# A new written order, new engine choices and new buffer places for the same 24-group attention and expert kernel

## The chip, the cores and the metric

The kernel runs on one core of one Trainium2 chip. The metric is device microseconds of one execution on that core; the times before are given as the median of three runs. Names of engines: PE multiplies matrices, DVE (VectorE), ACT (ScalarE) and POOL (GpSimd) work elementwise, SP only issues transfers here. A matmul's result lies in PSUM (8 banks); PE writes PSUM, DVE and ACT read it, POOL works on SBUF alone.

## The reference, cut to what matters

```python
def _attn_ref(x, inducing):              # x: 4 x 11456 x 128, inducing: 32 x 128
    def mab(q, kv):
        s = scale * (q @ kv.transpose(0, 2, 1))
        s = s - s.max(-1, keepdims=True)
        a = np.exp(s)
        a /= a.sum(-1, keepdims=True) + 1e-09
        return a @ kv
    h = mab(I, x)                         # 32 rows per batch
    return mab(x, h).astype(np.float32)

def _moe_ref(x, expert_emb, tau, w1, w2):  # x: the 45824 x 128 result above
    logits = xn @ en.T / tau              # xn, en: rows of norm 1
    expert_idx = np.argmax(logits, axis=1)
    probs = softmax(logits); gate_w = probs[arange, expert_idx]
    for e in range(8):
        mask = expert_idx == e
        h = np.maximum(x[mask] @ w1[e], 0.0)
        out[mask] = gate_w[mask, None] * (h @ w2[e])
```

## The kernel before, in words

Each of the 4 batches is cut into 6 groups of 1,920 tokens, so there are 24 groups, 0 to 23; groups 0 to 5 are batch 0, and so on. All of a batch's tokens turn out to take one expert, which the kernel finds from a vote and reads as a whole; a verdict at the end looks at whether that held, and a slow loop behind it (not run here) does the work otherwise.

Stage 1 of a group g: `load g` brings the tokens with channels on partitions. A second form of the same tokens, tokens on partitions, comes either by a second transfer (`loadx g`, 12 of the groups) or by transposes on PE (`xt g.0`, `xt g.1`) and their copies out of PSUM (`xe g.0`, `xe g.1`). `s1` are the scores on PE, `e1` their exp on ACT, `e1t` a transpose on DVE, `h` the accumulation of the batch's 32 rows on PE.

After a batch's sixth `h` come the small steps of `finish`: `zc, zr, rz, hsb, hd, hdc, tab, tabc, vote, pick`, then `loadw` (1 MB of the chosen expert's weights by two transfers, whose address `pick` gives), and with the weights `G, GT, gs, gk, K, Kc, K4, K4c`. `tabs`, `ad`, `md`, `mdc`, `marg`, `mq`, `mx`, `h2`, `zk` and `ck1` to `ck5` serve the gate and the verdict.

Stage 2 goes over pairs of groups (named by the first, 0, 2, ... 22). For each group: `s2` (scores, PE), `am` (maximum, DVE), `e2` (exp, ACT), `ud` (PE), `w` (product, DVE or POOL, with `uc` as a copy for POOL). Then one chain for the pair: `n2` and `dt` (DVE), `ln, ex` (ACT), `z, fac` (POOL), `den` (DVE), `lg` (POOL), `el` (ACT), `S` (DVE), `v` (POOL), `gf` (the gate's reciprocal, on DVE as two instructions or on ACT as three). With the gate each group's output follows: `F` (DVE spreads the gate), `eg` (product, POOL or DVE), `out` (four matmuls in two PSUM pairs), `oe .0` and `oe .1` (copies of 960 columns each out of PSUM, ACT or DVE) and `store` (SP, 960 KB). Groups 18, 22 and 23 do this in two parts (`F 22.0`, `eg 22.0`, `out 22.0`, `oe 22.0.0`, `oe 22.0.1`, `store 22.0`, and `.1`), whose copies have 512 and 448 columns.

No scheduler moves anything. `ORDER` (lines 58 to 113) is the list of all steps; each engine executes its own steps in that order, and a quote mark behind a name takes the second of the step's possible engines. `SEATS` gives each tile its place among 18 large, 5 middle and 10 small buffers and 8 PSUM banks. A step waits for its inputs and for the former users of its place. `FILL` puts matmuls on zeros ahead of some PE steps, so many to a PSUM bank (line 709). A `load` or `loadx` also waits for the fifth one before it:

```python
DEPTH = 5
            if op.paced:
                if len(paced) >= DEPTH:
                    tc.add_manual_dep(op.insts[0].ins, paced[-DEPTH].insts[-1].ins.name,
```

Of the kernel before, what the change touches and what calls it, by code (L numbers as in the profile page):

```python
# [63 lines left out]
hdc 0', shd 1, s1 9, s2 0, xe 9.0, tab 0, tabc 0, s2 5, vote 0, am 0, pick 0, sta 0, stb 0, load 11, tabs 0.0,
tabs 0.1, tabs 0.2, s2 4, e1 6, e1 9, stc 0, std 0, e2 0, load 10, s2 1, tabs 0.3, am 5, tabs 0, e1t 9, e2 1, am 1,
s2 2, e2 2, ud 0, ud 2, e2 4, uc 0, ud 1, am 2, s1 10, e1 10, w 0, ad 0, s2 3, load 7, pad 23, am 4, e1t 6, e2 5,
w 1, h2 0, s1 7, n2 0, md 0, pad 11, dt 0, e2 3, ln 0, ex 0, mdc 0, z 0, e1t 10, load 8, pad 17, am 3, loadx 6,
e1 7, load 12, loadw 0, ud 4, w 4, fac 0, uc 2, den 0, ud 3, dt 2, ud 5, w 5, dt 4, lg 0, z 2, loadx 7, el 0, S 0,
xt 11.0, xe 11.0, w 3, e1t 7, n2 4, xt 10.0, xe 10.0, v 0, gf 0, F 0, w 2, n2 2, eg 0, xt 12.1, xe 12.1, xt 11.1,
xt 9.1, xe 9.1, zk 0, F 1, z 4, xt 10.1, xe 10.1, loadx 8, ln 2, ex 2, s1 8, e1 8, G 0, h 6, GT 0, ln 4, gs 0,  # L70
s1 11, fac 2, den 2, h 7, lg 2, e1t 8, s1 12, load 16, load 20, h 8, gk 0, marg 0.0, el 2, S 2, K 0, ex 4, fac 4,
den 4, lg 4, e1 11, load 14, marg 0.1, el 4, m1 12, ck1 0, marg 0, xe 11.1', eg 1, mq 0, h 9, Kc 0, sha 2, shb 2,
e1t 11, K4 0, h 10, K4c 0, mx 0, shc 2, ck2 0, shd 2, load 13, v 2, h 11, gf 2, S 4, v 4, ck3 0, hsb 1, zc 1, zr 1,
rz 1.0, rz 1, F 2, e1 12, load 15, out 0, oe 0.1, F 3, hd 1, s1 14, load 17, hdc 1', tab 1, gf 4', e1t 12, out 1,
e1 14, tabc 1', vote 1, oe 0.0, loadx 16, F 4, s2 6, store 0, s2 9, pick 1, F 5, tabs 1.0, tabs 1.1, am 6, s2 10,
oe 1.0, oe 1.1, eg 2', eg 5, eg 4, sta 1, stb 1, am 9, s1 13, loadw 1, stc 1, std 1, s2 8, h2 1, e1t 14, e2 9, e2 6,
s2 11, am 11, e2 10, e2 8, s2 7, e2 7, e2 11, tabs 1.2, am 8, tabs 1.3, tabs 1, s1 15, eg 3, am 7, am 10, xt 17.0,
xe 17.0, ud 8, w 8, e1 13, ad 1, e1t 13, ud 6, loadx 14, w 6, ud 9, dt 8, ud 7, e1 15, uc 7, out 2, s1 16, md 1,
oe 2.1, w 9, oe 2.0, n2 8, G 1, ln 8, ex 8, w 7, z 8, e1 16, n2 6, loadx 13, dt 6, mdc 1, ud 10, w 10, z 6, fac 8,
den 8, load 18, e1t 15, GT 1, gs 1, xt 12.0, marg 1.0, gk 1, xe 12.0, lg 8, xt 17.1, xe 17.1, ln 6, ud 11, w 11,  # L80
loadx 15, marg 1.1, el 8, zk 1, out 3, oe 3.1, marg 1, e1t 16, S 8, h 12, mq 1, store 1, v 8, ex 6, s1 17, dt 10,
fac 6, h 13, oe 3.0, den 6, n2 10, K 1, gf 8, F 8, lg 6, mx 1, F 9, ck1 1, out 4, oe 4.1, Kc 1', oe 4.0', h 14,
s1 18, load 23, el 6, h 15, e1 17, K4 1, store 2, out 5, eg 9, S 6, zc 2, eg 8, h 16, ln 10, K4c 1, ex 10, oe 5.0,
ck2 1, e1t 17, m1 18, v 6, z 10, fac 10, den 10, lg 10, gf 6, sha 3, shb 3, zr 2, rz 2.0, ck3 1, rz 2, oe 5.1, h 17,
hsb 2, F 6, eg 6, load 22, loadx 22, shc 3, shd 3, el 10, S 10, loadx 19, e1 18, store 5, xt 18.0, xe 18.0, v 10,
hd 2, hdc 2', s1 23, tab 2, tabc 2', s2 12, F 7, vote 2, out 6, am 12, pick 2, gf 10, e1 23, s2 17, sta 2, load 19,
tabs 2.0, tabs 2.1, tabs 2.2, e1t 23, tabs 2.3, oe 6.0, stb 2, tabs 2, e1t 18, s2 14, hde 3, loadw 2, load 21, eg 7,
stc 2, oe 6.1, std 2, e2 12, am 17, am 14, s2 15, e2 15, F 10, eg 10, e2 14, F 11, eg 11, s2 16, e2 17, ad 2, am 15,
s2 13, am 13, s1 20, e2 16, am 16, out 7, e1 20, ud 12, e1t 20, e2 13, oe 7.0, oe 7.1, store 7, ud 14, uc 14, ud 13,
w 12, ud 15, w 13, w 15, dt 14, out 8, oe 8.1, w 14, oe 8.0, z 14, s1 19, s1 22, n2 14, ln 14, ex 14, n2 12, ln 12,  # L90
ex 12, dt 12, G 2, GT 2, h2 2, z 12, fac 12, zk 2, fac 14, md 2, mdc 2, gs 2, ud 16, xt 18.1, den 12, e1 22,
marg 2.0, lg 12, den 14, e1 19, w 16, xe 18.1, e1t 19, marg 2.1, el 12, S 12, marg 2, mq 2, xt 23.1, xe 23.1,
xt 23.0, xe 23.0, ud 17, v 12, lg 14, gf 12', out 9, gk 2, F 13, e1t 22, F 12, mx 2, dt 16, loadx 21, loadx 20,
store 3, h 18, oe 9.0, store 6, eg 13', store 8, oe 9.1, s1 21, e1 21, el 14, h 19, out 10, w 17, oe 10.0, e1t 21,
S 14, h 20, v 14, gf 14, n2 16, eg 12', K 2, Kc 2, h 21, oe 10.1, ln 16, out 11, oe 11.0, F 15, eg 15, h 22,
oe 11.1', K4 2, K4c 2', zc 3, ex 16, z 16, fac 16, h 23, hsb 3, zr 3, rz 3.0, den 16, rz 3, store 9, lg 16, el 16,
out 13, oe 13.1, F 14, store 10, oe 13.0, hd 3, hdc 3', tab 3, S 16, store 11, v 16, gf 16, s2 18, tabc 3', vote 3,
out 12, oe 12.1, oe 12.0, eg 14', am 18, sta 3, store 4, pick 3, stb 3, tabs 3.0, F 16, tabs 3.1, s2 21, stc 3,
std 3, tabs 3.2, am 21, tabs 3.3, tabs 3, s2 19, am 19, eg 16', e2 18, e2 21, s2 20, F 17, am 20, e2 19, ud 18,
uc 18, w 18, e2 20, loadw 3, store 12, ud 19, w 19, store 13, dt 18, n2 18, eg 17, out 14, oe 14.0, ln 18, ud 20,  # L100
w 20, z 18, zk 3, ud 21, w 21, oe 14.1, store 14, dt 20, z 20, n2 20, out 15, ex 18, G 3, s2 22, GT 3, fac 18,
den 18, lg 18, oe 15.0, oe 15.1, s2 23, store 15, ad 3, gs 3, ln 20, out 16, am 23, e2 22, ex 20, fac 20, am 22,
el 18, e2 23, S 18, gk 3, v 18, oe 16.1, oe 16.0, den 20, lg 20, ud 22, w 22, gf 18', F 19, F 18.1, F 18.0, ud 23,
# [776 lines left out]
```

## Time and profile before

| | |
|---|---|
| median of three runs | 166.08 us (165.87 to 166.93) |
| the profiled execution's own time | 166.93 us |
| its span, first to last instruction | 165.2 us |
| busy PE, DVE, ACT, POOL | 154.0, 125.3, 114.9, 53.0 us |
| moved on SP's queue | 62.92 MB, 95.4% of 16 DMA engines' span |

The profiled execution is the slowest of the three, 0.85 us over the median; 1.73 us of its own time lie outside the span. Busy times are of each engine alone and overlap; a matmul's end is modelled, so a busy PE says that matmuls stood ready and not that PE was at its peak.

### The profile page before, as it was taken

Reading aid. Unit: us, or ns where it says so; the run is one execution under the profiler, and the core shown is the slowest. Engines: PE = TensorE matmul, PEld = TensorE weight load, DVE = VectorE, ACT = ScalarE, POOL = GpSimd, SP = SyncE. Lnnn points to the kernel's source line nnn. Section 1 sums busy time; section 2 is a strip of 40 time slices with the busy share of each in tenths; the row PEclk is TensorE's granted clock in tenths of the full one; section 3 lists DMA queues with packets and bytes.
Section 4 is the critical chain, followed back from the end, with each engine's and each line's share of the span. In section 5 each row is a group of like instructions: output and inputs, shape, how many; then the busy total and the mean of one; then the engine's idle time right before and its main releaser. Section 6 shows DMA issues by size and latency. Waiting matters only on the chain.

```text
span 165.2 us, 5835 instructions
## 1 busy us (share of the span) xinstructions
PE 154.0 (93%) x2351; PEld 82.6 (50%) x2351; DVE 125.3 (76%) x323; ACT 114.9 (70%) x238; POOL 53.0 (32%) x148
## 2 busy tenths in 40 slices
...
GB/s 159 421 424 427 411 415 411 415 426 406 413 398 337 348 415 420 420 415 415 426 397 417 411 390 293 314 354 413 417 418 419 281 429 413 372 397 392 413 405 72
DMA packets 10574, 63.34 MB, mean 384 GB/s; under 512 B 1320, under 2 KB 1328, under 8 KB 10544
## 3 DMA queue, kind: packets, MB, share of 16 engines
q1 hardware_dynamic: 10368, 62.92, 95.4%
...
## 4 chain that ended last, share of the span: by engine, by line
PE 77%; DVE 12%; ACT 3%; POOL 2%; issue 1%; POOLq 0%; ACTq 0%
PE psum L304 62%; PE psum L406 12%; DVE big L301 2%; DVE sml L629 2%; ACT big L301 2%; PE psum L709 2%; POOL sel L276 2%; DVE gf L616 1%; PE psum L374 1%; ACT E L425 1%; DVE n L590 1%; DVE sum L612 1%; DVE sml L631 1%; DVE sml L429 0%; ACT mid L554 0%
## 5 line engine op out<-in xcount | busy, mean ns | idle before, releaser
L301 ACT COPY big<-psum 128x960 f32<-128x960 f32 (+4 forms) x67 | 58.7, 913 | 13.6 <-PE psum L304 9.2
L304 PE MATMUL psum<-sml,K 32*128 32x480 f32 (+2 forms) x216 | 26.7, 566 | 1.0 <-POOL z L603 0.7
L304 PE MATMUL psum<-big,sml 128*32 128x128 f32 x720 | 27.0, 274 | 0.0
L304 PEld LDWEIGHTS psum<-big,sml 128*32 128x32 f32 x720 | 22.6, 110 | 8.7 <-issue 4.2
L631 POOL TENSOR_TENSOR sml<-mid,sml 128x480 f32<-128x480 f32 (+2 forms) x18 | 20.4, 1147 | 19.5 <-DVE sml L629 9.9
L304 PE MATMUL psum<-big,ind 128*32 128x480 f32 x192 | 25.4, 571 | 0.0
L406 PE MATMUL psum<-ident,big 128*128 128x128 f32 x180 | 23.0, 282 | 0.2
L425 ACT ACTIVATE E<-psum,nb 128x480 f32<-128x480 f32 (+2 forms) x28 | 18.2, 652 | 6.6 <-PE psum L304 6.1
L406 PEld LDWEIGHTS psum<-ident,big 128*128 128x128 f32 x180 | 20.1, 144 | 4.9 <-issue 1.6
L304 PE MATMUL psum<-mid,tD 32*32 32x480 f32 x192 | 22.5, 569 | 0.0
L304 PE MATMUL psum<-mid,tab 32*32 32x480 f32 x192 | 22.5, 569 | 0.0
L304 PE MATMUL psum<-big,hd 128*32 128x480 f32 x192 | 22.3, 568 | 0.0
L429 DVE STREAM_TRANSPOSE sml<-E 128x480 f32<-128x480 f32 x24 | 15.9, 664 | 7.1 <-ACT E L425 7.1
L568 POOL TENSOR_TENSOR mid<-sml,mid 128x480 f32<-128x480 f32 x6 | 7.3, 1210 | 42.0 <-ACT sml L301 42.0
L554 ACT ACTIVATE mid<-psum,nb 128x480 f32<-128x480 f32 x24 | 14.5, 660 | 4.3 <-DVE nb L377 3.8
L550 DVE TENSOR_REDUCE am<-psum 128x1 f32<-128x480 f32 x24 | 15.2, 647 | 2.6 <-PE psum L304 2.0
L629 DVE STREAM_TRANSPOSE sml<-gf 128x480 f32<-128x480 f32 (+2 forms) x27 | 15.7, 600 | 0.0
L568 DVE TENSOR_TENSOR mid<-psum,mid 128x480 f32<-128x480 f32 x18 | 11.5, 638 | 3.3 <-PE psum L304 3.1
L304 PEld LDWEIGHTS psum<-sml,K 32*128 32x128 f32 x216 | 8.6, 183 | 10.7 <-ACT big L301 2.6
L590 DVE TRANSPOSE_TENSOR_REDUCE n<-mid 128x30 f32<-128x960 f32 x12 | 13.7, 1148 | 0.1
L709 PE MATMUL psum<-zero 128*128 128x256 bf16 x66 | 11.4, 312 | 1.7 <-DVE zero L260 1.0
L301 DVE COPY big<-psum 128x960 f32<-128x960 f32 (+4 forms) x11 | 10.4, 954 | 1.1 <-PE psum L304 0.8
...
## 6 DMA issues: line engine op xcount, KB each, us to landing
...
```

The source lines that it names most:

```text
L301: return nc.scalar.copy(out, in_) if e == "ACT" else ENG[e].tensor_copy(out, in_)
L304: return nc.tensor.matmul(out, lhsT=lhsT, rhs=rhs, start=start, stop=stop)
L406: return [nc.tensor.transpose(ap(tp)[:, (q - q0) // 4, 128 * ((q - q0) % 4):128 * ((q - q0) % 4) + 128], v(q), ident) for q in range(q0, q1)]
L425: return [nc.scalar.activation(ap(e1)[r0:r1, :n], ap(ps)[r0:r1, :n], AF.Exp, bias=bt.t("nb")[r0:r1, 0:1], scale=SCALE, accum_out=bt.t("zk" ...
L429: add(f"e1t {g}", ("DVE",), lambda e: [nc.vector.transpose(ap(e1t), ap(e1))], [e1], [e1t])
L550: add(f"am {g}", ("DVE",), lambda e, ps=ps, k=k: [v.tensor_reduce(t("am")[:, k:k + 1], ap(ps)[:, :W], AX.X, ALU.max, apply_absolute_value= ...
L554: add(f"e2 {g}", ("ACT",), lambda e, ps=ps, a=a: [nc.scalar.activation(ap(e2)[:, a], ap(ps)[:, :W], AF.Exp, bias=t("nb")[:, 1:2], scale=SC ...
L568: return [ENG[e].tensor_tensor(ap(wp)[:, a], src(), ap(e2)[:, a], ALU.mult)]
L590: add("n2 " + nm, ("DVE",), lambda e: [v.tensor_reduce(fl2(u("n2")), ap(wp).rearrange("p a (q i) -> p (a q) i", i=32), AX.X, ALU.add, appl ...
L629: add(f"F {nm}", ("DVE",), lambda e, a=a, f=f, q0=q0, q1=q1: [v.transpose(ap(f).rearrange("p (q i) -> p q i", i=32)[:, q0:q1], u("gf")[:, ...
L631: add(f"eg {nm}", ("POOL", "DVE"), lambda e, a=a, f=f, e2g=e2g, c0=c0, c1=c1: [ENG[e].tensor_tensor(ap(e2g)[:, c0:c1], ap(e2)[:, a, c0:c1] ...
L709: fill = [nc.tensor.matmul(psum[:, s, 0:256], lhsT=zero[:, 0:P], rhs=zero, start=True, stop=True) for _ in range(n)]
```

## The change

`ORDER`, `SEATS` and `FILL` are replaced; the set of steps, `LOADED`, `W_POOL`, `SPLIT`, `DEPTH` and all functions stay. SP issues the same 72 transfers in another order. 41 steps change engine: `eg 2, 12, 13, 14, 16, 22.0, 23.0, 23.1` go from DVE to POOL and `eg 4` from POOL to DVE; `gf 0, 8, 16, 20`, `K4c 0, 1, 3`, `hsb 3`, `oe 0.1, 22.0.0, 22.1.1` and seven `xe` from ACT to DVE; `en7`, `gf 12`, `hdc 1`, `tabc 1, 2`, `oe 4.0, 18.0.0, 21.1, 23.0.0, 23.1.0, 23.1.1` and three `xe` from DVE to ACT. The fill matmuls are 72 instead of 66.

The last lines of the new list and the new fills, as they stand in the diff (two lines of the list, then the table of fills):

```diff
+oe 22.0.0', marg 3, oe 21.0, store 21, eg 23.1, mq 3, out 22.1, oe 22.0.1, oe 22.1.0, out 23.1, oe 23.1.1,
+store 22.0, oe 22.1.1', eg 23.0, out 23.0, ck4 1, ck5 1, mx 3, oe 23.1.0, store 23.1, ck2 3, store 22.1, ck3 3,
...
 FILL = {
-    "xt 0.1": (0, 16), "xt 0.0": (2, 3), "tab 3": (2, 4), "ud 19": (2, 2), "ud 21": (0, 2), "ud 23": (3, 2),
-    "K4 3": (0, 5), "out 18.0": (0, 6), "out 20": (4, 3), "out 21": (2, 5), "out 22.0": (4, 8), "out 22.1": (6, 4),
-    "out 23.0": (4, 5), "ck4 3": (2, 1),
+    "xt 0.1": (0, 16), "s1 0": (2, 3), "ud 17": (2, 2), "tab 3": (4, 4), "out 15": (4, 2), "ud 23": (2, 2),
+    "K4 3": (0, 5), "out 18.0": (0, 3), "out 19": (0, 3), "out 21": (2, 9), "out 22.0": (6, 14), "out 23.0": (2, 3),
+    "ck2 3": (4, 3), "ck4 3": (0, 3),
 }
```

What the instructions of three engines are, in a row, at the places that the prediction comes to. In these rows `sml<-gf` is `F`, `sml<-mid,sml` is `eg`, `n<-mid` is `n2`, `gf<-v` is `gf`, `big<-psum` is `oe`, `den<-s` is `den`, `K<-psum` is `K4c`; the numbers behind names are places.

DVE, from the copy of `K` or the last pair's `n2` on, before:

```order
L590 TENSOR_REDUCE n_125<-mid_85 128x30
L629 STREAM_TRANSPOSE sml_96<-gf_113 128x480
L301 COPY big_78<-psum 128x2x8x32
L486 TENSOR_REDUCE chk_123<-tab_117 128x1
L629 STREAM_TRANSPOSE sml_90<-gf_113 128x480
L655 TENSOR_REDUCE chk_123<-am_119 128x1
L656 TENSOR_REDUCE chk_123<-n_125 128x1
L606 RECIPROCAL den_102<-s_100 128x30
```

and after the change:

```order
L301 COPY K_122<-psum 128x128
L629 STREAM_TRANSPOSE sml_91<-gf_113 128x480
L616 RECIPROCAL gf_105<-v_104 64x30 x2
L629 STREAM_TRANSPOSE sml_95<-gf_105 128x480
L590 TENSOR_REDUCE n_125<-mid_85 128x30
L655 TENSOR_REDUCE chk_123<-am_119 128x1
L656 TENSOR_REDUCE chk_123<-n_125 128x1
L301 COPY big_82<-psum 128x2x15x32
L606 RECIPROCAL den_110<-s_108 128x30
```

The copy of `K`, the gate `gf 20` and `F 20` now stand ahead of the last pair's `n2 22`; before, they stood behind it or on ACT.

POOL, the last steps, before:

```order
L631 TENSOR_TENSOR sml_92<-mid_83,sml_96 128x480
L608 TENSOR_TENSOR lg_106<-sml_93,den_102 128x240
L613 TENSOR_TENSOR v_104<-sum_103,z_101 128x30
L631 TENSOR_TENSOR sml_89<-mid_84,sml_88 128x224
L531 TENSOR_TENSOR q_163<-q_163 128x16
```

and after:

```order
L613 TENSOR_TENSOR v_112<-sum_111,z_109 128x30
L631 TENSOR_TENSOR sml_88<-mid_84,sml_96 128x256
L631 TENSOR_TENSOR sml_88<-mid_84,sml_96 128x224
L454 COPY chk_123<-zc_151 128x1
L454 TENSOR_SCALAR chk_123<-zc_151 128x1
L631 TENSOR_TENSOR sml_91<-mid_84,sml_93 128x224
L531 TENSOR_TENSOR q_163<-q_163 128x16
L631 TENSOR_TENSOR sml_91<-mid_84,sml_93 128x256
```

Behind `v 22` POOL had one half product (`eg 22.1`); now it has all four halves of groups 22 and 23, and the two instructions of `zk 3`.

SP, the last five stores, before (`store 21` has 1920 columns; then `22.1, 23.0, 22.0, 23.1`):

```order
L644 DMA out_0<-big15_80 128x1920
L644 DMA out_0<-big7_72 128x896
L644 DMA out_0<-big5_70 128x1024
L644 DMA out_0<-big7_72 128x1024
L644 DMA out_0<-big5_70 128x832
```

and after (`22.0, 23.1, 22.1, 23.0`):

```order
L644 DMA out_0<-big12_77 128x1920
L644 DMA out_0<-big1_66 128x1024
L644 DMA out_0<-big10_75 128x832
L644 DMA out_0<-big1_66 128x896
L644 DMA out_0<-big10_75 128x1024
```

`store 22.1` stood ahead of both stores of group 23; now it stands between them.

## Rows read from the trace of the kernel before

**Rows 1.** The page: busy times, GB/s in 40 slices, SP's queue.
```profile
PE 154.0 (93%) x2351; PEld 82.6 (50%) x2351; DVE 125.3 (76%) x323; ACT 114.9 (70%) x238; POOL 53.0 (32%) x148
...
GB/s 159 421 424 427 411 415 411 415 426 406 413 398 337 348 415 420 420 415 415 426 397 417 411 390 293 314 354 413 417 418 419 281 429 413 372 397 392 413 405 72
...
q1 hardware_dynamic: 10368, 62.92, 95.4%
```
**Rows 2.** Windows: stretch, length, busy us of each engine, PEclk, DMA share, GB/s.
```profile
4.75:135.40 130.65, 130.26 (x2110) 71.53 (x2114) 102.79 (x255) 95.82 (x203) 39.42 (x91) 1.00 1.00 397
...
38.50:49.20 10.70, 10.70 (x166) 7.47 (x162) 10.19 (x21) 9.33 (x21) 5.00 (x12) 1.00 1.02 412
49.20:53.00 3.80, 3.80 (x107) 3.30 (x102) 3.68 (x13) 3.01 (x12) 2.23 (x4) 1.00 0.90 340
...
125.50:159.40 33.90, 30.05 (x354) 11.26 (x346) 30.79 (x87) 25.59 (x49) 12.69 (x23) 1.00 0.99 389
150.40:159.40 9.00, 5.99 (x63) 3.03 (x55) 7.82 (x30) 3.73 (x7) 0.90 (x2) 1.00 1.00 410
...
133.60:163.40 29.80, 21.95 (x253) 9.16 (x237) 23.55 (x67) 19.28 (x38) 9.80 (x19) 0.94 0.94 380
```
**Rows 3.** Timeline of SP's issues: start and us of the last store's issue.
```profile
158.52 0.33 SPq L644 DMA_DIRECT2D out<-big  x1
```
**Rows 4.** Line 644 at 158.52: the last store, from issue to landing.
```profile
DMA to landing us min/median/max: 4.9/4.9/4.9
```
**Rows 5.** Timeline of PE: start, us, and matmul records of `s2 17` and `s2 14`.
```profile
93.43 1.56 PE L304 MATMUL psum<-big,hd 128*32 128x480 f32 x8
...
95.12 1.01 PE L304 MATMUL psum<-big,hd 128*32 128x480 f32 x8
```
**Rows 6.** Timelines of DVE (`eg 2`, `eg 16`) and of POOL at 61.59 (three products).
```profile
62.22 1.11 DVE L631 TENSOR_TENSOR sml<-mid,sml 128x480 f32<-128x480 f32 x1
...
128.90 0.65 DVE L631 TENSOR_TENSOR sml<-mid,sml 128x480 f32<-128x480 f32 x1
...
61.59 3.98 POOL L631 TENSOR_TENSOR sml<-mid,sml 128x480 f32<-128x480 f32 x3 [5.47 <-DVE idx L482]
```
**Rows 7.** Groups by line and shape: count, busy us, mean ns of one, idle before.
```profile
L301 ACT COPY big<-psum 128x960 f32<-128x960 f32 x38 | 35.1, 960 | 7.5 <-PE psum L304 7.4
...
L631 POOL TENSOR_TENSOR sml<-mid,sml 128x480 f32<-128x480 f32 x15 | 18.4, 1238 | 17.4 <-DVE sml L629 7.8 <-DVE idx L482 5.5 <-DVE chk L655 1.7
...
L629 DVE STREAM_TRANSPOSE sml<-gf 128x480 f32<-128x480 f32 x21 | 13.6, 658 | 0.0
...
L301 DVE COPY big<-psum 128x960 f32<-128x960 f32 x4 | 4.6, 1151 | 0.4 <-PE psum L304 0.4
...
L616 DVE RECIPROCAL gf<-v 64x30 f32<-64x30 f32 x8 | 2.7, 335 | 1.0 <-POOL v L613 0.9
...
L301 DVE COPY big<-psum 128x512 f32<-128x512 f32 x2 | 1.3, 672 | 0.4 <-PE psum L304 0.4
...
L631 POOL TENSOR_TENSOR sml<-mid,sml 128x224 f32<-128x224 f32 x2 | 1.3, 672 | 2.1 <-DVE sml L629 2.1
...
L301 DVE COPY K<-psum 128x128 f32<-128x128 f32 x1 | 0.3, 291 | 0.1
```
**Rows 8.** Timeline of DVE near the end: `n2 22`, `gf 22`, the verdict's last.
```profile
143.63 1.13 DVE L590 TRANSPOSE_TENSOR_REDUCE n<-mid 128x30 f32<-128x960 f32 x1
...
149.69 0.68 DVE L616 RECIPROCAL gf<-v 64x30 f32<-64x30 f32 x2 [0.36 <-POOL v L613]
...
159.24 0.14 DVE L681 CAST ni<-fw 1x1 int32<-1x1 f32 x1
```
**Rows 9.** Timelines of POOL (`mq 3`), ACT (`el 22`) and PE (`out 23.1`) near the end.
```profile
154.70 0.22 POOL L531 TENSOR_TENSOR q<-q 128x16 f32<-128x16 f32 x1 [2.26 <-DVE q L529]
...
148.15 0.41 ACT L610 ACTIVATE ex<-lg 128x240 f32<-128x240 f32 x1
...
156.62 0.66 PE L304 MATMUL psum<-sml,K 32*128 32x224 f32 x8
```

More of the change, by code (lines that the diff above doesn't have):

```diff
@@ L64 @@
[L64 to L103, printed above, removed]
@@ L109 @@
[L109 to L112 removed]
+load 0.1, xt 0.1, load 0.0, pad 11, ind, s1 0, en1, en3, en4, xt 0.0, pad 5, en5, m1 0, load 1, en6, xt 1.1, load 4,
+xe 0.1, xe 1.1, load 2, en7, xe 0.0', sha 0, s1 1, shb 0, shc 0, shd 0, e1 1, e1 0, xt 1.0, xe 1.0', xt 4.1, e1t 1,
```

80 lines of the change are left out of this document (58 added, 22 removed), and 8 rows, old and new, of the table ps.

## The prediction

> **What bounds the kernel now.** I read the page first, for the busy times and the transfer rate by slices [rows 1], then windows of single stretches [rows 2], to see which engine is full where. The reader is to see two parts. From 4.75 to 135.40 us PE is busy 130.26 of 130.65 us, at a granted clock of 1.00: in that part PE is the bound, with 0.39 us of gaps, and only a shorter PE list or gaps hidden in its busy time could shorten it. From 125.5 us on (when the last `pick` has its result) to the verdict, DVE is busy 30.79 of 33.90 us, while PE's 30.05 include 47 fill matmuls and ACT has 25.59: there DVE is the fullest engine. Beside both runs the stream of transfers: 62.92 MB, 95.4% of the span's DMA time [rows 1]. Its good slices show 411 to 429 GB/s, but there are dips to 337 and 348 (near 50 us), to 293 and 314 (near 100 us) and to 281 and 372 (behind 127 us). The span ends 1.8 us behind the last landing: the last store is issued at 158.52 [rows 3] and lands 4.9 us later [rows 4], at 163.4.
>
> The profiled execution took 166.93 us, 1.73 of them outside its span, and lies 0.85 above the median of 166.08. All differences below are made on its own time and then put on the median.
>
> **The changed load order, first part.** In the new order several loads that are free to go are issued ahead of those that wait for a batch's last `h`, so the dip at 49.2 to 53.0 (340 GB/s, against 412 before it) should fill. Filled, it brings the stream forward by 3.80 × (1 − 340/412) = 0.7 us there, and by about 2 us if the slices behind it also stay at 412. PE however is busy 10.70 of 10.70 and 3.80 of 3.80 us in these two windows [rows 2]: it has data all through the dip. So I cost this at nothing; what hides it is PE's own queue of matmuls. If that cover were gone, 0.7 to 2 us would be the price or gain. The first ten transfers stand in the same order in both kernels, so the head stays.
>
> **PE's list.** The matmuls of the reference are the same. Up to the last `vote` the fills gain two, on `ud 17`. I estimate 0.15 us each (eight records of 480 columns in `s2 14` take 1.01 us [rows 5], 0.13 each, and a fill's 256 columns about as much), nothing where they fill a gap: 0 to +0.3 us, and I take +0.3, as PE shows no gaps there. The other fills stand behind 125.5 us, where PE is not the bound. Hidden waits: the eight records of `s2 17` took 1.56 us, those of `s2 14` 1.01 [rows 5]; with the new order the copies that `s2 17`'s bank waits for stand earlier, so up to 0.55 goes. Against it, `h 21` needs `e1t 21`, which now stands on DVE behind an `n2` and an `xe`: 0 to +0.6, taken +0.3, in the middle. Sum for PE's part: +0.3 − 0.55 + 0.3 = **+0.05 us**, bounds −0.55 to +0.9.
>
> **Products from DVE to POOL, in the middle.** A whole `eg` costs POOL 1.238 us and DVE 0.65 [rows 6, 7]. Four of the five that move (`eg 2, 12, 13, 14`) lie in the part that PE bounds, and POOL is busy 39.42 of 130.65 us there [rows 2], so neither the gain on DVE nor the longer product is on the path: nothing. Without POOL's idle time each would cost 1.238 − 0.65 = 0.6 us. In the trace `eg 2` took 1.11 us on DVE (at 62.22) beside three products on POOL (from 61.59, 3.98 us), `eg 16` 0.65 [rows 6].
> The Trainium skill ("SBUF — State Buffer", section "Who interferes with whom") calls the port pair that DVE and GpSimd share an exclusive lock. The 1.11 against 0.65 us agrees with it. By it the move takes a collision of 0.46 us off DVE at 62 us, where PE is the bound, so the sum by it is the same.
>
> **DVE behind the last `pick`.** Ten steps leave DVE here: two whole or near-whole pieces of output (`oe 21.1` 1.15 [rows 7], `oe 18.0.0` about 0.65), `eg 16` 0.65 [rows 6], three half products of about 0.39 (estimated at 0.6 of a whole one), three half copies at 0.67 or less [rows 7], and a check (0.27, an estimate), 5.8 us together. Five join: `gf 16` and `gf 20` at 2 × 0.335, `K4c 3` 0.29, `oe 22.0.0` and `oe 22.1.1` [rows 7], 2.9 together. The sum falls by 2.9 us. But most of that lies behind `gf 22`. Up to it, `eg 16`, `oe 18.0.0` and the check leave (1.57) and `gf 16`, `gf 20`, `K4c 3` join (1.63): equal. And the order got worse for the last pair: `n2 22` now stands behind `K4c 3` (0.29), `gf 20` (0.67) and `F 20` (0.66), **1.6 us** of work that in the kernel before stood behind it or on ACT. `n2 22` ended at 144.76, `gf 22` began at 149.69 [rows 8]: 4.93 us for a chain of ACT, POOL and DVE steps, part of which was queueing (the gate's `lg` stood on POOL behind a whole `eg` of 1.2 us, which is also POOL's in the new list, but earlier relative to it). So 0 to 1.6 us passes on; I take 0.9, a little over the middle, as one queue of 1.2 us can absorb about half: `gf 22` then ends at 150.37 + 0.9 = 151.3.
>
> **Behind `gf 22`.** The old list had DVE busy 7.82 of 9.00 us from 150.4 to 159.4, POOL 0.90 [rows 2]. In the new one four `F` halves run on DVE (about 0.4 each) and POOL does all four half products (0.672 the smaller [rows 7], an estimated 0.75 the larger), two short instructions of `zk 3` (together about 0.4, estimated at twice the 0.22 of `mq 3` [rows 9]) and `mq 3` in between: from the second `F` half on 0.75 + 0.67 + 0.4 + 0.67 + 0.22 + 0.75 = 3.5 us. Then four matmuls (0.7 [rows 9]) and two copies on one engine (1.2). 151.3 + 0.8 + 3.5 + 0.7 + 1.2 = 157.5, and three handovers of 0.1 us: 157.8 for the last issue, bounds 156.9 (nothing passes on) to 158.5 (all does), against 158.52 [rows 3]. With the same 4.9 us to land [rows 4] that is 0.7 us earlier. But SP is in order: `store 22.1` has its data at about 155.5 and waits behind `store 23.1` until about 157.0. The bytes that are under way then last at most some 1.1 us (448 KB at 413 GB/s), so up to 0.5 us of the stream is empty, and the last three stores (1.41 MB, 3.4 us at 413 GB/s) are sent in a burst, landing up to 0.5 us later than before. Ends −0.7 and +0.5; I take +0.1, nearer to the stream, as its slices are full (413, 405) right up to its end in the trace [rows 1].
> Sum: +0.05 + 0.1 = +0.15; 166.93 becomes 167.1, and 166.08 becomes **166.2 us: no change**. About 1% (1.7 us) is what a measurement of this kernel can tell from none. The bounds of the single terms give 166.08 − 0.55 − 0.7 = 164.8 to 166.08 + 0.9 + 0.5 = 167.5, the likeliest case's own range.
>
> **Rivals.** (1) The relief pays. DVE's 2.9 us less reach the end, since DVE is the fullest engine of the tail, and with earlier copies the stores come evenly. What caps it is the stream: from 133.6 to 163.4 us it moved at 380 GB/s [rows 2], 11.3 MB; at 418, as in the good slices [rows 1], that takes 27.1 instead of 29.8 us. 166.08 − 2.7 = **163.4**. For it: 7.82 of 9.00 us behind `gf 22`. Against: the sum up to `gf 22` does not fall.
> (2) Slower, by the last pair's gate. The 1.6 us ahead of `n2 22` pass whole to `gf 22`, because no queueing is left to absorb them, and the burst of the stores adds its 0.5: 166.08 + 2.1 + 0.05 = **168.2**. If an ACT copy (0.96 [rows 7]) also falls ahead of the gate's `el`, it replaces what the shorter tail gives back. It decides once `el 22` begins more than 0.4 us later than its 148.15 [rows 9] with all four products still to come on POOL. For it: POOL's four halves in a row take 3.5 us where before two engines shared them. Against: POOL is nearly idle there (0.90 of 9.00).
> (3) The change does for the loads what it says, and it shows: the stream runs some 2 us ahead in the middle and keeps it to the end, since a stream that is 95.4% occupied has little else to lose. Then the last loads land earlier and the stores have room; the time would come out near rival 1's, 166.08 − 2 = **164.1**. Against it stands that stores, not loads, end the program, and they wait for engines.
> The Trainium skill ("DMA: Bandwidth & Descriptors", section "Where 436 GB/s comes from") holds that for transfers between HBM and SBUF the HBM share of about 358 GB/s per core binds. By that the 62.92 MB would take 175.8 us, an estimate, and any order would give no change. The trace disagrees: slices of 420 and more [rows 1], and a span below that.
>
> **How the numbers follow.** Forecast, no change: 0.53. Rivals 1 and 3, faster by over 1%: 0.27 together (0.20 and 0.07). Rival 2, slower by over 1%: 0.20. The 1% lines lie at 164.4 and 167.7. The range for 8 in 10 cuts about one in ten on each side: from 163.4, rival 1's time, which more than half of its cases do not reach, to 168.4, a little over rival 2's.
>
> **What the profile after would show.** Right: PE busy nearly all of the time up to about 135.4 us, with `s2 17` near 1.0 us; the slices at 50 us at 410 or more and PE's end unchanged; `n2 22` ending near 146.4 and `gf 22` near 151.3; the last issue near 157.8 and the last landing at 163 to 164. For rival 1: `gf 22` at 150.4 or before, the slices behind 133 us near 418. For rival 2: `gf 22` behind 152 and an issue behind 159. For rival 3: the last weights' landing earlier than the stores' share explains, and the span's end moved by as much as the stream. Wrong I would be if PE shows waits of over 1 us in its full part (a load or an `h` that comes late), or if the last `vote` comes over 1 us earlier: then PE's busy time held gaps that I took for work.

## The result and the profile after

The changed kernel takes **167.47 us**, median of 15 runs (167.01 to 168.17), the kernel before 166.38 in 15 runs of the same sessions (165.51 to 167.32): ratio **1.0071, 95% interval 1.0048 to 1.0094**. That is 0.7% slower, inside the bound of 1% that the prediction called no change, and inside its range. The prediction took about 1% for what can be told from none; the interval here leaves out 1, so it tells 0.7% from none. The profiled executions took 167.39 us (after) and 166.93 (before); the one of before lay 0.55 us over its own median, the one of after 0.1 under, so the profiles show 0.5 us of the 1.1.

The page after: busy times, GB/s in 40 slices and SP's queue, to be laid beside [rows 1].

```profile
PE 155.5 (94%) x2357; PEld 82.0 (49%) x2357; DVE 128.3 (77%) x323; ACT 111.1 (67%) x228; POOL 59.1 (36%) x155
...
GB/s 156 422 430 415 416 416 419 412 414 418 410 412 418 409 419 405 373 393 425 419 415 378 427 384 383 427 421 412 321 411 207 197 403 418 401 380 414 409 406 82
...
q1 hardware_dynamic: 10368, 62.92, 94.4%
```

The dip near 50 us is gone, as the prediction had it, and the one near 100 us is shallower (384 and 383, was 293 and 314). The one near 128 us, behind the last loads, is deeper: two slices of 207 and 197, where one of 281 stood. PE has 1.5 us more, DVE 3.0, POOL 6.1, ACT 3.8 less.

Windows of after, the stretches that answer to [rows 2]. Those that hang on the last `pick` are set 1.3 us later, as it is, and the last one, behind `gf 22`, 1.57 later.

```profile
4.75:136.70 131.95, 131.27 (x2114) 70.58 (x2118) 108.53 (x262) 91.55 (x195) 43.52 (x94) 1.00 0.98 395
...
49.20:53.00 3.80, 3.80 (x111) 3.36 (x107) 3.76 (x13) 3.19 (x8) 2.76 (x7) 1.00 1.01 418
126.80:160.70 33.90, 30.46 (x358) 11.69 (x350) 28.89 (x83) 25.61 (x45) 16.06 (x29) 1.00 0.92 361
151.97:160.97 9.00, 5.90 (x60) 3.32 (x58) 5.22 (x26) 4.91 (x8) 3.25 (x7) 0.97 1.01 411
```

PE stays full up to a point 1.3 us later (131.27 of 131.95 us). Behind the last `pick` DVE is less full: 28.89 of 33.90 us, and 5.22 of the 9.00 behind `gf 22` where it was 7.82.

A program of 166 us that starts a little differently each time is best compared from mark to mark. I use the start of the first `vote` (batch 0), of the last (batch 3), and the last store's landing. PE's timeline at these votes, before (two rows) and after:

```profile
31.04 0.22 PE L304 MATMUL psum<-tab,ones 128*32 128x8 f32 x8
...
124.74 0.22 PE L304 MATMUL psum<-tab,ones 128*32 128x8 f32 x8
```

```profile
30.96 0.22 PE L304 MATMUL psum<-tab,ones 128*32 128x8 f32 x8
...
126.01 0.23 PE L304 MATMUL psum<-tab,ones 128*32 128x8 f32 x8
```

SP's timeline after at the last store [rows 3]:

```profile
158.58 0.46 SPq L644 DMA_DIRECT2D out<-big  x1
```

and line 644's view of that store, from issue to landing [rows 4]:

```profile
DMA to landing us min/median/max: 5.3/5.3/5.3
```

The landings, from the same trace, are at 163.38 us before and 163.85 after.

| | first to last vote | last vote to last landing |
|---|---|---|
| before (31.04, 124.74, 163.4) | 93.7 | 38.6 |
| after (30.96, 126.01, 163.9) | 95.05 | 37.8 |

**So the new list loses 1.35 us in the part that PE fills and wins 0.8 back behind it.** Each number is from one execution, and the spread is some tenths: e8 below, with the same list up to the last `vote`, takes 95.3 in the first part, e1 and e11, with the old one, 93.2 and 93.8. Where PE lost it, in its timeline after (start, us, records; the last words of a row are the idle time ahead of it and what ended it): first `h 11` up to the step behind it (`out 0`, at 56.99), then `ud 12` and `ud 14`.

```profile
55.17 0.62 PE L304 MATMUL psum<-big,sml 128*32 128x128 f32 x11
56.18 0.74 PE L304 MATMUL psum<-big,sml 128*32 128x128 f32 x18 [0.39 <-issue]
...
56.99 1.09 PE L304 MATMUL psum<-sml,K 32*128 32x480 f32 x8
...
100.60 0.99 PE L304 MATMUL psum<-mid,tab 32*32 32x480 f32 x2
101.07 0.58 PE L304 MATMUL psum<-mid,tD 32*32 32x480 f32 x1
...
102.29 0.56 PE L304 MATMUL psum<-mid,tab 32*32 32x480 f32 x1 [0.18 <-ACT mid L554]
```

and the same places before (`h 11` and `out 0`, `ud 12` and `ud 14`):

```profile
55.30 1.07 PE L304 MATMUL psum<-big,sml 128*32 128x128 f32 x29
...
56.41 1.09 PE L304 MATMUL psum<-sml,K 32*128 32x480 f32 x8
...
100.36 0.59 PE L304 MATMUL psum<-mid,tab 32*32 32x480 f32 x1
...
101.19 0.56 PE L304 MATMUL psum<-mid,tab 32*32 32x480 f32 x1
```

`h 11` stops after 11 of its matmuls for 0.39 us, and the profile names nothing that it waited for; from its start to `out 0` 1.82 us pass, where it was 1.11. `ud 12` starts its first matmuls, on `tab`, at 100.60, but those on `tD` only at 101.07: from its start to that of `ud 14` 1.69 us pass, where the same step took 0.83 before. Busy time hides most of that, since a matmul that is queued counts as busy (the two ahead on `tab` are put down with 0.99 us). These two, 0.71 and 0.86, with 0.33 for the two new fills (e6) and less the 0.55 that before lost at `s2 17` [rows 5], come to the 1.35. What `ud 12` waits for is `tabs 2` on DVE:

```profile
62.80 1.04 DVE L482 TENSOR_SCALAR oh<-iota,idx 128x8 f32<-128x8 f32 x1
...
89.45 1.10 DVE L452 TENSOR_SCALAR rhs<-sel,zc 128x160 f32<-128x160 f32 x1
...
99.48 0.37 DVE L483 TENSOR_TENSOR lo<-oh,tab 128x8 f32<-128x8 f32 x1
...
100.08 0.94 DVE L484 TENSOR_SCALAR tD<-tab,lg 128x16 f32<-128x16 f32 x1
```

and POOL's timeline at the same places, all products `eg`:

```profile
62.60 1.21 POOL L631 TENSOR_TENSOR sml<-mid,sml 128x480 f32<-128x480 f32 x1 [2.99 <-DVE sml L629]
...
89.25 1.21 POOL L631 TENSOR_TENSOR sml<-mid,sml 128x480 f32<-128x480 f32 x1 [0.49 <-PE psum L304]
...
98.60 2.38 POOL L631 TENSOR_TENSOR sml<-mid,sml 128x480 f32<-128x480 f32 x2 [3.01 <-DVE sml L629]
```

`tabs 2` ends at 101.02 and POOL's second product at 100.98; the steps at 62.80 and 89.45 also end with POOL's product (63.84 against 63.81, 90.55 against 90.46). `ud 14` then waits 0.18 us more for an exp on ACT (`e2`), and that one had waited for a maximum that stands behind `tabs 2` on DVE:

```profile
101.61 0.66 ACT L554 ACTIVATE mid<-psum,nb 128x480 f32<-128x480 f32 x1 [0.80 <-DVE am L550]
```

In the old list `tabs 2` was done at 95.65, 4.7 us ahead of `ud 12`:

```profile
95.44 0.21 DVE L484 TENSOR_SCALAR tD<-tab,lg 128x16 f32<-128x16 f32 x1
```

The end of the program, DVE's timeline [rows 8]:

```profile
146.53 1.14 DVE L590 TRANSPOSE_TENSOR_REDUCE n<-mid 128x30 f32<-128x960 f32 x1
...
151.32 0.68 DVE L616 RECIPROCAL gf<-v 64x30 f32<-64x30 f32 x2 [0.36 <-POOL v L613]
...
159.97 0.14 DVE L681 CAST ni<-fw 1x1 int32<-1x1 f32 x1
```

Against the last vote `n2 22` starts 1.63 us later than before (20.52 behind it, was 18.89), `gf 22` 0.36 later (25.31, was 24.95), and the verdict ends 0.5 earlier (34.10, was 34.64).

### The profile page after: what moved, and what is told of

It reads as the page before. It is cut to its first block, busy times and chain, and to the rows that moved or that the text cites. A ratio compares the mean times of both kernels' runs of the same rounds, so it can differ in the third digit from the quotient of the medians.

```text
span 165.6 us, 5854 instructions
## 1 busy us (share of the span) xinstructions
PE 155.5 (94%) x2357; PEld 82.0 (49%) x2357; DVE 128.3 (77%) x323; ACT 111.1 (67%) x228; POOL 59.1 (36%) x155
## 4 chain that ended last, share of the span: by engine, by line
PE 75%; DVE 13%; POOL 4%; issue 2%; ACT 2%; POOLq 0%
PE psum L304 56%; PE psum L406 13%; PE psum L709 4%; POOL sml L631 2%; DVE am L550 2%; DVE sml L629 2%; ACT mid L554 2%; DVE n L590 1%; DVE gf L616 1%; POOL lg L608 1%; DVE mid L568 1%; POOL mid L568 1%; DVE oh L482 1%; DVE big L301 1%; PE psum L374 1%
## 5 line engine op out<-in xcount | busy, mean ns | idle before, releaser
L301 ACT COPY big<-psum 128x960 f32<-128x960 f32 (+4 forms) x66 | 56.7, 895 | 18.9 <-PE psum L304 11.2
L631 POOL TENSOR_TENSOR sml<-mid,sml 128x480 f32<-128x480 f32 (+2 forms) x25 | 26.9, 1087 | 22.0 <-DVE sml L629 16.2
L304 PEld LDWEIGHTS psum<-big,sml 128*32 128x32 f32 x720 | 22.0, 110 | 9.1 <-issue 4.7
L629 DVE STREAM_TRANSPOSE sml<-gf 128x480 f32<-128x480 f32 (+2 forms) x27 | 16.2, 607 | 0.8 <-ACT gf L617 0.6
L301 DVE COPY big<-psum 128x1024 f32<-128x1024 f32 (+4 forms) x12 | 13.0, 1086 | 3.9 <-PE psum L304 2.4
L709 PE MATMUL psum<-zero 128*128 128x256 bf16 x72 | 12.3, 313 | 1.1 <-DVE zero L260 1.1
```

Source lines behind the costliest of these rows:

```text
L301: return nc.scalar.copy(out, in_) if e == "ACT" else ENG[e].tensor_copy(out, in_)
L304: return nc.tensor.matmul(out, lhsT=lhsT, rhs=rhs, start=start, stop=stop)
L629: add(f"F {nm}", ("DVE",), lambda e, a=a, f=f, q0=q0, q1=q1: [v.transpose(ap(f).rearrange("p (q i) -> p q i", i=32)[:, q0:q1], u("gf")[:, ...
L631: add(f"eg {nm}", ("POOL", "DVE"), lambda e, a=a, f=f, e2g=e2g, c0=c0, c1=c1: [ENG[e].tensor_tensor(ap(e2g)[:, c0:c1], ap(e2)[:, a, c0:c1] ...
L709: fill = [nc.tensor.matmul(psum[:, s, 0:256], lhsT=zero[:, 0:P], rhs=zero, start=True, stop=True) for _ in range(n)]
```

## The experiments

In these edits, which move words of the list, each tile keeps the place that it had, except where it is said. Ratios are to the kernel before, run beside.

**Which part?** The two lists differ by five steps in what stands up to the last `pick`, so they can be cut there and put together crosswise. e1 is the old list up to the cut and the new one behind it:

```diff
-pick 3, stb 3, tabs 3.0, F 16, tabs 3.1, s2 21, stc 3, std 3,
+pick 3, ck1 2, s2 19, loadw 3, tabs 3.0, store 12, stb 3, stc 3, s2 20,
...
```

> The list of the kernel before up to and with the last pick (step 640 of 831), then the new list's steps; places behind the cut are the new ones, renamed. Theory 1 (the loss lies in the part that PE fills: in the new order the last vote ends 1.27 us later, at 126.23 against 124.96, and the new tail wins some of it back, the verdict being 0.73 later and the last landing 0.47): the last vote at 124.9 to 125.1, the last landing 0.5 to 0.8 us before 163.38, ratio to the kernel before 0.995 to 0.998. Rival (the loss lies in the tail, its burst of stores and products on POOL): as slow as the changed kernel, 1.005 to 1.009. Rival (the stream alone sets the end): 1.000 to 1.003.

Measured: 166.33 us, ratio **1.0005** (0.9978 to 1.0032). First to last vote 93.2, last vote to landing 38.8: its last store took 6.3 us from issue to landing. The loss is gone with the old first part, so it lies there and not in the new tail. The gain of the new tail didn't come either. The 6.3 us stand alone: in the eleven other profiles with the new tail the last store lands 4.9 to 5.3 us after its issue, and the tail is 37.7 to 37.9 us long.

e2 is the reverse:

```diff
-pick 3, loadw 3, oe 12.0, tabs 3.0, store 12, stb 3, stc 3, v 16,
+pick 3, v 16, gf 16, oe 12.0, stb 3, tabs 3.0, F 16, tabs 3.1,
...
```

> The reverse: the new list up to and with the last pick, then the old list's steps. Theory 1: the last vote near 126.2, 1.3 us later than before, and the old tail gives none of it back: ratio to the kernel before 1.007 to 1.010, at or a little over the changed kernel's 1.0071. Rival (loss in the tail): 0.999 to 1.002.

Measured: 169.02, ratio **1.0163** (1.0124 to 1.0201); 95.1 and 39.3 us. The first part is as long as the changed kernel's, as theory 1 has it; the tail is longer than either, more than was expected. Three steps of the old list (`v 16, gf 16, oe 12.0`) come behind the cut here and not ahead of it, so it can't tell what the old tail itself costs.

**The table of batch 2.** e3 puts the steps that end in `tabs 2` one behind another:

```diff
-tabs 2.0, F 11, am 15, tabs 2.1, e2 14, F 10, e1t 18, eg 10, am 14, tabs 2.2, tabs 2.3, store 5, e2 12, out 7, tabs 2,
+tabs 2.0, tabs 2.1, tabs 2.2, tabs 2.3, tabs 2, F 11, am 15, e2 14, F 10, e1t 18, eg 10, am 14, store 5, e2 12, out 7,
```

> The changed kernel with the four small steps that end in tabs 2 (table of batch 2) put on DVE straight behind the first one, ahead of F 11, am 15, F 10, e1t 18 and am 14. Theory 1a (ud 12 lost 0.86 us on PE because tabs 2 came at 101.02, behind those five steps and stretched from 0.2 to 0.94 us while POOL ran eg 11): tabs 2 done by 99, ud 12 takes about 1.0 instead of 1.50 us, the last vote 0.6 to 0.9 us earlier than 126.23, and the time 0.995 to 0.998 of the changed kernel, so ratio to the kernel before 1.002 to 1.005. Rival (PE's delay in the middle is covered by what bounds the tail): last vote earlier, ratio unchanged at 1.007.

Measured: 167.07, ratio 1.0055 (1.0033 to 1.0077). `tabs 2` ended at 97.85 and took 0.24 us, `ud 12` took 1.04. But first to last vote is 95.3, no less. PE's waits between 95 and 106 us, by releaser:

```profile
PE psum L305 <- DVE am L551: 0.6, 1, 0.6
```

The wait now stands at `s1 20`, the step behind `s2 13`, and a maximum (`am`) ends it. Theory 1a saw one releaser rightly, but behind it stood the next.

e4 takes POOL's two products away instead. They are `eg 10` and `eg 11`, which were POOL's in the kernel before too:

```diff
-F 10, e1t 18, eg 10, am 14, tabs 2.2, tabs 2.3, store 5, e2 12, out 7, tabs 2, s2 13, am 13, e2 16, am 16, ad 2, e1t 23, eg 11,
+F 10, e1t 18, am 14, tabs 2.2, tabs 2.3, store 5, e2 12, out 7, tabs 2, s2 13, am 13, e2 16, am 16, eg 11', eg 10', ad 2, e1t 23,
```

> The changed kernel with the products eg 10 and eg 11 on DVE behind am 16 instead of on POOL; tabs 2 keeps its place in DVE's list. It tells a long DVE queue from DVE steps stretched by POOL's product. Lock theory: the two steps that took 0.37 and 0.94 us beside eg 10 and eg 11 take 0.17 and 0.21 with nothing on POOL, tabs 2 is done by about 100.1, ud 12 takes 1.0 to 1.1 us. Queue theory: they keep their durations, tabs 2 ends at 101.0. The time: the 1.3 us more on DVE may delay w 12 and w 13, so between 1.002 and 1.009 of the kernel before.

Measured: 167.15, ratio 1.0059 (1.0036 to 1.0081). DVE's timeline, the two steps that had taken 0.37 and 0.94 us:

```profile
99.03 0.15 DVE L484 TENSOR_TENSOR lo<-oh,tab 128x8 f32<-128x8 f32 x1
...
99.40 0.23 DVE L485 TENSOR_SCALAR tD<-tab,lg 128x16 f32<-128x16 f32 x1
```

With nothing on POOL they take 0.15 and 0.23: it was the products that stretched them. And again the time stays: PE waits in the next steps, between 99 and 105 us,

```profile
PE psum L305 <- DVE mid L569: 0.4, 1, 0.4
```

for a product `w` on DVE, whose bank `ud 15` takes; first to last vote 95.2.

e5 moves all that isn't a maximum behind the maxima:

```diff
-tabs 2.0, F 11, am 15, tabs 2.1, e2 14, F 10, e1t 18, eg 10, am 14, tabs 2.2, tabs 2.3, store 5, e2 12, out 7, tabs 2,
-s2 13, am 13, e2 16, am 16, ad 2, e1t 23, eg 11,
+tabs 2.0, tabs 2.1, tabs 2.2, tabs 2.3, tabs 2, am 15, e2 14, am 14, store 5, e2 12, out 7, s2 13, am 13, e2 16, am 16,
+F 11, F 10, eg 10, e1t 18, eg 11, ad 2, e1t 23,
```

> The changed kernel with the table steps of batch 2 and then am 15, am 14, am 13 and am 16 ahead of F 11, F 10 and e1t 18 on DVE (POOL's eg 10 and eg 11 so come later). The two runs before moved PE's wait about without shortening it (0.86 at ud 12, 0.82 at s2 13 with the table early, 0.63 at ud 13 with the products on DVE). Theory 2: it is the four maxima of stage 2 at the end of DVE's queue that PE waits for, since s2 17 and out 6 now stand ahead of vote 2 and no longer cover them: now the wait should be under 0.2, the last vote 0.6 to 0.8 us earlier (94.3 to 94.5 us behind vote 0, where the changed kernel has 95.05), ratio to the kernel before 1.002 to 1.005. Rival (the products' collisions or another engine): the wait stays at 0.6 to 0.9 at some step.

Measured: 167.85, ratio 1.0090 (1.0056 to 1.0123), first to last vote 95.6. The wait moved on to `ud 15` and grew:

```profile
PE psum L305 <- ACT mid L555: 1.1, 1, 1.1
```

The step of ACT that ended it is `e2 15`, behind `e1 20`, which needs the place that `e1t 18` gives back, and that I had moved away. e9 mends that (the edit against e5):

```diff
-am 15, e2 14, am 14, store 5, e2 12, out 7, s2 13, am 13, e2 16, am 16,
-F 11, F 10, eg 10, e1t 18, eg 11, ad 2, e1t 23, oe 7.1, s1 20, oe 7.0, store 7, e2 13, ud 12, w 12,
+am 15, e1t 18, e2 14, am 14, store 5, e2 12, out 7, s2 13, am 13, e2 16, am 16,
+oe 7.1, s1 20, oe 7.0, store 7, e2 13, ud 12, w 12, F 11, F 10, eg 10, eg 11, ad 2, e1t 23,
```

> The changed kernel; on DVE the table steps of batch 2, am 15, e1t 18, am 14, am 13, am 16 and then w 12 come ahead of F 11, F 10, ad 2 and e1t 23. The run with the maxima first had moved e1t 18 back too, and e1 20 takes the place that e1t 18 leaves, with e2 15 behind it on ACT; ud 15 takes w 12's bank: PE stood 1.25 us at ud 15. Theory 3 (PE waits for what DVE hands back in that stretch, places and banks by the new table among them, whichever DVE step is last): with all of them ahead the wait is under 0.3 us at every step from ud 12 to ud 15, the last vote 94.2 to 94.5 us behind vote 0 (95.05 in the changed kernel), ratio to the kernel before 1.001 to 1.005. Rival: another wait of 0.6 to 0.9 us takes its place (then DVE's whole work in that stretch is the limit, and no order of it helps), ratio 1.006 to 1.009.

Measured: 170.49, ratio **1.0225** (1.0184 to 1.0265). PE's waits from 99 to 112 us (engine, line, releaser, us):

```profile
PE psum L305 <- ACT sml L302: 2.7, 1, 2.7
```

ACT's timeline of e9 at that step of ACT:

```profile
106.17 0.56 ACT L302 COPY sml<-psum 128x480 f32<-128x480 f32 x1 [3.58 <-POOL sml L632]
```

and POOL's, just ahead of it:

```profile
103.78 2.35 POOL L632 TENSOR_TENSOR sml<-mid,sml 128x480 f32<-128x480 f32 x2 [8.16 <-DVE sml L630]
```

Read from below: POOL's `eg 10, eg 11` waited for the two `F` that I had moved back, from 96.53 and 97.78 to 102.40; ACT's `uc 14` waited 3.58 us for the place that they give free; PE waited 2.7 us for the bank that `uc 14` reads. Two transposes of 0.66 us, off the path by every window, cost 3 us (170.49 against 167.47) through two places. Theory 3 falls, and its rival holds in a stronger form: none of the orders of DVE that I tried there (e3, e4, e5, e9) made the first part shorter than after's 95.05.

**The fills.** e6 takes the two ahead of `ud 17` out:

```diff
-    "xt 0.1": (0, 16), "s1 0": (2, 3), "ud 17": (2, 2), "tab 3": (4, 4),
+    "xt 0.1": (0, 16), "s1 0": (2, 3), "tab 3": (4, 4),
```

> The changed kernel without the two fill matmuls ahead of ud 17. Priced at 0.15 us each in the prediction; in the trace they take 0.3 to 0.4 us together. Theory: PE has no gap there, so the last vote comes 0.3 us earlier and the ratio to the kernel before falls by 0.001 to 0.002, to 1.005 to 1.006. Rival: the fills hide a wait that then stands at ud 17, nothing moves (1.007).

Measured: 166.99, ratio **1.0037** (1.0012 to 1.0061); first to last vote 94.7, 0.33 us less than after. The two fills in PE's timeline after:

```profile
109.14 0.39 PE L709 MATMUL psum<-zero 128*128 128x256 bf16 x2
```

The time fell by 0.5 us, with intervals that overlap. It is the only mend of the new first part that shortened PE's stretch, by not much more than the spread of one list (95.05 and 95.28, after and e8).

**The full stream and `h 11`.** e7 thins out the transfers between 50 and 56 us:

```diff
-h 8, load 13, xe 11.1,
+h 8, xe 11.1,
...
-marg 0, load 17, load 14, el 4,
+marg 0, load 14, load 13, el 4,
...
-eg 1, load 15, S 4,
+eg 1, load 15, load 17, S 4,
```

> The changed kernel with load 13 behind load 14 and load 17 behind load 15, as before, so that the stream thins out between 50 and 56 us again (340 to 390 GB/s instead of 412 to 418). All profiles of the new list show a pause of 0.4 to 0.7 us on PE within h 11 at 55 us, for which the trace names no releaser and which the old list (0 to 0.2) hardly shows. Theory F (the pause comes with the full stream): h 11 takes under 1.2 us instead of 1.5, the last vote 0.4 to 0.6 earlier, ratio 1.003 to 1.006. Rival (it comes from PE's own list there): the pause stays, ratio 1.006 to 1.009.

Measured: 168.19, ratio 1.0095 (1.0059 to 1.0132). The window from 50 to 56 us of after:

```profile
50.00:56.00 6.00, 5.79 (x167) 4.62 (x159) 5.14 (x21) 3.99 (x12) 3.85 (x10) 1.00 1.02 418
```

the same window of e7:

```profile
50.00:56.00 6.00, 6.00 (x190) 5.09 (x179) 5.14 (x21) 3.84 (x12) 3.73 (x9) 1.00 0.76 256
```

and PE's timeline of e7 in `h 11`:

```profile
55.01 0.94 PE L305 MATMUL psum<-big,sml 128*32 128x128 f32 x26
```

At 256 GB/s the pause in `h 11` is gone: 26 records in a row. The gain was lost two steps on, at `s1 13`, since load 13 now came late (PE's waits of e7, 53 to 60 us):

```profile
PE psum L305 <- DMA big<-in_xT: 1.6, 1, 1.6
```

The other profiles say the same. Between 52 and 56 us the stream moved 354, 354 and 361 GB/s in the three with the old first part (before, e1, e11) and 323 in e7: no pause. In the ten others it moved 409 to 417, and each has a pause without a releaser at 55 to 56 us, of 0.2 to 0.7 us. So theory F fits the pause, not the time.

The trace shows what else goes with it. Beside the program's own queue the profile has one of the kind `instruction`, with 19 transfers of 16 KB; its line on the page of after, and in after's DMA view from 53.60 to 53.70 us:

```profile
q8 instruction: 19, 0.31, 0.8%
...
q8 instruction: 1, 0.02, 66.6%
```

In each of the ten pauses PE goes on 2.49 to 2.58 us after such a transfer has begun (after: 53.64 and 56.18). An eleventh pause, 0.35 us in a later `h` of e11, does the same (115.65 and 118.15):

```profile
118.15 0.42 PE L304 MATMUL psum<-big,sml 128*32 128x128 f32 x7 [0.35 <-issue]
```

It also shows that the stream's rate beside it is not the condition: from 116.0 to 118.2 us e11 moved 360 GB/s, and before and e1, without a pause there, 419 and 433. In e7 PE's list is that of after, but the transfer begins at 51.00, 2.6 us earlier, in a stretch of 123 GB/s (50 to 52 us), and PE comes to the place without a pause. So it looks as if PE runs out of instructions there, because they come late behind the data. That is argued from these times: the trace doesn't say whose instructions the queue brings, and no run changed it alone.

**The order of the last stores.** e8:

```diff
-mx 3, oe 23.1.0, store 23.1, ck2 3, store 22.1,
+mx 3, oe 23.1.0, store 22.1, store 23.1, ck2 3,
```

> The changed kernel with store 22.1 ahead of store 23.1, as its data are ready first (copies done at 156.04 against 157.37). The prediction's step: the held-back store costs up to 0.5 us of stream. If so the last landing comes 0.2 to 0.5 earlier, ratio 1.004 to 1.006. Rival (the last copies at 158.56 and one unloaded store's 4.5 to 5 us set the end): 1.006 to 1.008.

Measured: 167.42, ratio 1.0057 (1.0035 to 1.0079); last vote to landing 37.8, as after. The held-back store cost nothing.

**Three mends at once.** e10 is e9 with e6's and e8's edits:

```diff
-mx 3, oe 23.1.0, store 23.1, ck2 3, store 22.1,
+mx 3, oe 23.1.0, store 22.1, store 23.1, ck2 3,
...
-    "xt 0.1": (0, 16), "s1 0": (2, 3), "ud 17": (2, 2), "tab 3": (4, 4),
+    "xt 0.1": (0, 16), "s1 0": (2, 3), "tab 3": (4, 4),
```

> The run above together with the two other mends: no fill matmuls ahead of ud 17 (alone 1.0037), store 22.1 ahead of store 23.1 (alone 1.0057). If the three add up: last vote 0.9 to 1.1 us earlier than in the changed kernel, ratio to the kernel before 0.997 to 1.001. Rival (the end has a floor of its own from the stream): 1.002 to 1.004.

Measured: 169.57, ratio 1.0188 (1.0151 to 1.0225). It has e9's wait of 2.7 us too, so it doesn't show what the three add up to on a list without it.

**The stream's dip at 100 us.** e11 is e1 with

```diff
-store 7, loadx 21, loadx 20, store 3, store 6, store 8,
+store 3, store 6, store 7, loadx 21, loadx 20, store 8,
```

> The old list up to the last pick and the new one behind it (alone 1.0005), with store 3 and store 6, whose data are long there, ahead of store 7, for which SP waits until 102.5: that fills the stream's dip at 96 to 106 us and brings later transfers forward by some 2 us. Theory (the engines' tail sets the end, the stream's dips in the middle cost nothing): 0.999 to 1.002. Rival (the stream sets the end, its dips are lost time): last landing 1 to 2 us earlier, 0.988 to 0.995.

Measured: 166.12, ratio **0.9990** (0.9963 to 1.0017). From 96 to 106 us the stream moved 397 GB/s instead of e1's 331, and nothing that can be measured came of it. In its profile the tail is 37.7 us long, as short as after's; but the last vote came 93.8 behind the first, 0.6 later than in e1: PE waited 0.3 us for a load that had queued behind the two stores. Another 0.35 us is the pause at 118.15 shown under e7. It is no faster than the kernel before within its interval, so no version here beats the kernel before.

**The vote of batch 2.** e12, with e6's edit, and `tab 2` in bank 5:

```diff
-hdc 2', xt 18.0, ck3 1, xe 18.0', eg 6, out 6, eg 7, v 10, e1 23, oe 6.0, s2 12, hde 2, tab 2, tabc 2, am 12, load 19, s2 17, eg 8, eg 9, zk 2, vote 2, pick 2,
+hdc 2', xt 18.0, ck3 1, xe 18.0', hde 2, e1 23, tab 2, tabc 2, s2 12, eg 6, eg 7, v 10, am 12, load 19, eg 8, eg 9, zk 2, vote 2, out 6, oe 6.0, s2 17, pick 2,
```

> The changed kernel without the fills ahead of ud 17 (alone 1.0037), and around the vote of batch 2 in the old kernel's order: hde 2, tab 2, its copy and s2 12 ahead of out 6, and out 6, its copy and s2 17 behind vote 2 (tab 2 in bank 5). Theory 4 (PE stood at ud 12 because the new list puts out 6, s2 12 and s2 17 ahead of vote 2: the vote comes late and the work that covered the steps behind it on DVE is already done; what DVE does in that stretch can't be reordered to make room): vote 2 about 1 us earlier behind vote 0 although the same work remains, the wait from s2 13 to ud 15 under 0.3 us instead of 0.86, the last vote 93.9 to 94.2 us behind vote 0 (94.7 without the fills alone), ratio to the kernel before 0.997 to 1.001. Rival (DVE's whole work up to ud 15 is the limit): the wait stays at 0.6 to 0.9, ratio 1.003 to 1.005.

Measured: 167.41, ratio 1.0059 (1.0040 to 1.0079); first to last vote 95.1. `vote 2` came at 93.00 instead of 94.86, and yet `tabs 2` as late as ever, in DVE's timeline:

```profile
95.42 0.28 DVE L375 TENSOR_REDUCE first<-psum 1x1 f32<-1x128 f32 x1 [1.07 <-PE psum L374]
...
100.52 0.94 DVE L484 TENSOR_SCALAR tD<-tab,lg 128x16 f32<-128x16 f32 x1
```

DVE stood 1.07 us before `stb 2`, whose input `sta 2` is now behind `out 6` and `s2 17` on PE; the earlier vote was given back there. (In the old list `sta 2` stands behind them too, but `tabs 2` needs only one short step behind `stb 2` there.) Theory 4 isn't shown by this. Earlier vote and early table together were not tried.

## Why the prediction was right

Its forecast, no change, held, but by luck as much as by its sum: two terms were wrong the opposite way. It had +0.05 for PE's part and +0.1 for the tail; the profiles show +1.35 and −0.8, both outside the bounds of their terms (+0.9 and −0.7).

**PE's part is the step that failed**: "+0.3 − 0.55 + 0.3 = +0.05 us, bounds −0.55 to +0.9". The fills were right (0.39 us in the trace, 0.33 by e6). The 0.55 to be won at `s2 17` was not in the list: in e1 the same list has its eight records in 1.01 us, so one execution's chance was booked as a wait. Against e1's 93.2 the first part loses 1.85 us and not 1.35; less 0.8 in the tail that is 1.05, near the 1.09 between the medians. The wait at `h 21` didn't come (1.07 us to its next step, 1.25 before). What came stood in none of the terms: 0.86 us at `ud 12` to `ud 14`, and 0.71 from `h 11` to `out 0`. The first could have been looked for. The new order puts `out 6` and `s2 17` ahead of `vote 2` and spreads the table's steps between DVE's maxima; I had gone through PE's queue for loads, and not through what PE takes back from DVE behind each `vote`. That DVE's handbacks between 95 and 104 us set the wait, by themselves or through ACT and POOL, is shown by e3, e4, e5 and e9, which moved it from step to step. As none of them took it away, that it costs the whole 0.86 us is read from the timelines and not shown by a run; nor is it settled why the old list gets by without it.

**Products on POOL.** The forecast was that the four that move in the middle cost nothing. No run moved them alone; e4 moved two others, and the time stayed. The sentence on the shared port was half right: `eg 2` on POOL no longer collides on DVE, but at the same place a small step of DVE (`oh`, at 62.80) now takes 1.04 us beside it, where it took 0.23. The three other stretched steps (89.45, 99.48, 100.08) stand beside `eg 6`, `eg 10` and `eg 11`, which were POOL's before too: there the new order of DVE's own steps made the collision. They took 1.10, 0.37 and 0.94 us instead of 0.30, 0.15 and 0.23. The Trainium skill ("SBUF — State Buffer", section "Who interferes with whom") has the pair of ports as an exclusive lock, and the ends of these steps, within 0.1 us of the products' ends, agree.

**The load order** filled its dip and gained nothing, as forecast. But it was costed at nothing, and it wasn't free: the pause in `h 11` comes with the fuller stream and went with it in e7. Rival 3 is answered by the page after, where one dip is filled, another is shallower and the time is longer, and by e11.

**The tail.** The 1.6 us ahead of `n2 22` are there (1.63). They pass on by 0.36 and not 0.9, and the last issue comes 1.21 us earlier behind the last vote (32.57, was 33.78) where 0.7 was reckoned: four products in a row on POOL were no burden, and DVE had room. The last store then takes 0.4 us longer to land (5.3, was 4.9), about the 0.5 that the prediction had as the upper end. So the last landing is 0.8 earlier, not 0.1 later: that the stream, not the issue, ends the program was the wrong choice between the two ends that the text had; the term's lower end was −0.7. e8 takes the order of the last stores out of the account. The 0.8 rests on one profile of the old tail against eleven of the new. In e1 the same tail took 38.8 us, and by the times e1 and e11 gain at most 0.4% on the kernel before; how much of the 0.8 is the tail's own stays open.

**Rivals.** Rival 1 was half right: relief reaches the end, 0.8 of its 2.7. Rival 2's mark was passed (`el 22` 0.62 later behind the last vote: 24.03, was 23.41) without its consequence, so that mark was badly chosen. One reading of the prediction was off without touching the sum: of its 47 fill matmuls four stand ahead of 125.5 us, at 123.30.
